# Own probability buffers for six attention units, a later first weight join, a slot table in two parts, and narrow slots scaled by VectorE

## The chip, the cores and the metric

The kernel runs on one core of a Trainium2 chip. The metric is the device time of one execution in microseconds (us). The engines are named as the profile names them: PE is TensorE's matrix multiply and PEld its weight load, DVE is VectorE, ACT ScalarE, POOL GpSimd, SP SyncE, which here only issues transfers. An engine carries out its instructions in the order in which they stand in its program; between engines only semaphores hold them.

## The reference

Three stages follow one another, on 2304 tokens of 512 values, in float32.

```python
scores = 0.125 * (q @ k.T)             # 4 batches x 8 heads, 576 x 576, head size 64
mask   = local (32 back) for heads 0-3, every 32nd position for heads 4-7
attn   = softmax(where(mask, scores, -1e9)) / (sum + 1e-9);  x = attn @ v
xn     = x / sqrt(mean(x*x) + 1e-6) * rms_g
x      = (silu(xn @ w_gate) * (xn @ w_val)) @ w_out           # 512 -> 1536 -> 512
logits = x @ w_gate2 + modality_bias[modality_id]             # 8 experts
e, p   = argmax(logits), softmax(logits)[argmax]
out    = p * (relu(x @ w1[e]) @ w2[e])                        # 512 -> 1024 -> 512
```

## The kernel before, in words

**Attention** is cut into 48 units (a batch, two heads, a group of blocks). `attention(u)` has four steps: `scores()` (matmuls L195 into a PSUM bank; DVE adds the mask and writes the probability buffer `pr`, L206; DVE takes the maxima, L214; ACT takes the exponent in place, L217), `norm()` (DVE: sum L237, reciprocal L240, product L241), `transpose()` (PE L247, into PSUM, and a copy) and `output()` (PE L258). `pr` comes from a pool of three buffers: the unit three further on can write its own only when PE has transposed this one. GpSimd writes a small constant into the last column of each `pr` (L184).

The first twelve units run ahead of all else (the loop over `aux`). In this prologue the weights of the first feed-forward are loaded and converted as well. 36 weights of 512 KB come packed by the ACT queue (`load_w`, L446) and are taken apart in three steps: `conv_a` (GpSimd takes the middle bits, L452), `conv_b` (DVE joins them in place, L456; the "join") and `conv_c` (ACT rounds the high part, L463, DVE subtracts to get the low part, L464). Weight 3f is the gate of hidden block f, 3f+1 the value, 3f+2 the output. `convert()` takes the next of these steps from a list; in the prologue it starts after step P1 of `aux`.

**First feed-forward.** Tokens go in nine chunks of 256. After a normalisation (`rms`: L367 to L403; y, xh, xl at L413 to L417), `gate_val` does 24 matmuls for each hidden block (L511 to L513), `gelu_post` is ACT and DVE (L519 to L525), `ff_out` six matmuls (L536 to L538), two blocks behind. Chunk 1 starts two blocks behind chunk 0 and takes the same weights. The scheduler of the framework sets the order of each engine's rows by priorities; the rest of the attention is strewn between.

**Router and sorted experts.** For the last chunk and all that follows, `tc.manual_schedule()` keeps the order as written. `route_s` ranks the tokens (its last matmul is L631), `route_g` builds `ab` on DVE (L662, L665), and `route_i` is four matmuls on `ab` (L677) and an addition (L681) that give the sorted token numbers. `tables()` (DVE) works out from the counts which expert and which rows each of the slots t = 1 to 15 has: the rows in `s_l` (L971 to L984), the expert numbers in `ei` (`tables2()`, L990 to L1006). `gather(t)` turns `s_l` into row numbers (DVE L1034 to L1043) and fetches the tokens (GpSimd L1046); `experts(t)` reads `ei`. The work of a slot is `mm1` (L1098 to L1100, a relu at L1109 and L1115 behind it) and `mm2` (L1128 to L1138); `split` parts the loaded weights (ACT h L1062, DVE l L1063). `finish(t)` scales the result by the router's probability and writes it out. Slots 1, 7, 8 and 9 are narrow (192 rows instead of 256); in their second block ACT copies half of the PSUM tile, DVE adds the other half (L1154) and ACT scales (L1155). The last slot (`half_pair`, L1190) has its own relu `rl` (L1204) on ACT, which PE waits for at L1210.

Of the kernel before, what the change touches and what calls it, by code (L numbers as in the profile page):

```python
# [52 lines left out]
def moe_kernel(  # L53
# [117 lines left out]
    def attention(u, banks):  # L171
# [7 lines left out]
        def scores():  # L179
            t = qkv_t.pop((u, 0))  # L180

            pr = pp.tile([128, 4, LK + 1], F32, tag="pr", name="pr", bufs=3)
            if u < 12:
                G.memset(pr[:, :n, nk:nk + 1], 1e-9)  # L184
            mx = sm.tile([128, 4], F32, tag="mx", name="mx")
            sd = sm.tile([128, 4], F32, tag="sd", name="sd")
            sps = banks("s")
            if 0 < u < 12:
                fill(sps[:, 384:], 10)
            sps = sps[:, :4 * LK].rearrange("p (t k) -> p t k", k=LK)  # L190
# [12 lines left out]
            first = 1 if local and g == 0 else 0  # L203
            for i0, i1, mask in ((0, first, m_loc0), (first, n, m_loc if local else m_str)):
                if i1 > i0:
                    V.scalar_tensor_tensor(  # L206
                        out=pr[:, i0:i1, :nk],
                        in0=sps[:, i0:i1, :nk],
                        scalar=-0.125,
                        in1=mask[:, :nk].unsqueeze(1).to_broadcast([128, i1 - i0, nk]),  # L210
                        op0=ALU.mult,
                        op1=ALU.add,
                    )
            V.tensor_reduce(out=mx[:, :n], in_=pr[:, :n, :nk], op=ALU.min, axis=AX.X)  # L214
            for i in range(n):
                pv = pr[:, i, :nk]
                act = A.activation(  # L217
                    out=pv,
                    in_=pv,
                    func=AF.Exp,  # L220
                    bias=mx[:, i:i + 1],
                    scale=-1.0,
                    accum_out=None if u < 12 else sd[:, i:i + 1],
                )
                if not flow_on:
                    mark[0] = act
# [240 lines left out]
    mark = [None]  # L467
    flow_on = []

    def next_load():  # L470

        if n_wl[0] < NP and mark[0] is not None:
            with tc.issue_after(mark[0].ins):
                load_w(n_wl[0])
            n_wl[0] += 1

    conv = [lambda: conv_a(0), lambda: conv_b(0)]
    for n in range(1, NP):
        conv += [lambda n=n: (conv_a(n), conv_c(n - 1)), lambda n=n: conv_b(n)]
    conv += [lambda: conv_c(NP - 1)]  # L480
# [398 lines left out]
    def first_tables():  # L879
# [30 lines left out]
    def tables():  # L910
        tl, ti, r, h, nx = (lt[n] for n in ("tl", "ti", "r", "h", "nx"))
        wd, excl, incl, u = (lt[n] for n in ("wd", "excl", "incl", "u"))
        w0, w1, s_l, ex, place = (lt[n] for n in ("w0", "w1", "s_l", "ex", "place"))
        hi = lt["m"][:, 2:3]
        iota1 = iota[:, 1:E + 1]
        wide = [128, NL, 2, E]
        t_b = place.unsqueeze(2).unsqueeze(3).to_broadcast(wide)

        def before(a):
            V.tensor_tensor(out=ex, in0=lt["lt"], in1=a.unsqueeze(1).to_broadcast([128, E, E]), op=ALU.mult)  # L920
# [47 lines left out]
        yield  # L968
        V.tensor_tensor(out=u, in0=lt["base"], in1=excl, op=ALU.subtract)
        yield  # L970
        V.tensor_tensor(out=w0, in0=excl.unsqueeze(1).to_broadcast(wide), in1=t_b, op=ALU.is_le)  # L971
        yield
        V.tensor_tensor(out=w1, in0=incl.unsqueeze(1).to_broadcast(wide), in1=t_b, op=ALU.is_gt)
        yield
        V.tensor_tensor(out=w0, in0=w0, in1=w1, op=ALU.mult)
        yield

        V.scalar_tensor_tensor(
            out=w1, in0=u.unsqueeze(1).to_broadcast(wide), scalar=-float(BIG), in1=w0, op0=ALU.add, op1=ALU.mult
        )  # L980
# [6 lines left out]
    def tables2():  # L987
        w0, w1, et, ei, m = (lt[n] for n in ("w0", "w1", "et", "ei", "m"))
        wide = [128, NL, 2, E]
        V.tensor_tensor(  # L990
            out=w1, in0=w0, in1=lt["e_l"].unsqueeze(1).unsqueeze(2).to_broadcast(wide), op=ALU.mult
        )
        yield
        V.tensor_reduce(out=et[:, 1:], in_=w1.rearrange("p t a e -> p t (a e)"), op=ALU.add, axis=AX.X)
        yield
        V.tensor_scalar(out=et[:, 1:], in0=et[:, 1:], scalar1=m[:, 1:2], scalar2=None, op0=ALU.add)
        yield
        V.tensor_copy(et[:, 0:1], m[:, 1:2])
        yield
        V.tensor_copy(ei[:, 0], et[:, 1:])  # L1000
        yield
        V.tensor_tensor(out=ei[:, 1], in0=et[:, 1:], in1=et[:, :NL], op=ALU.not_equal)
        yield
# [139 lines left out]
    def finish(t, blocks=(0, 1), halves=False):  # L1143
        go = lt[f"go{t % 2}"]
        for m in blocks:
# [5 lines left out]
            elif m and t in NARROW:  # L1151
                A.copy(y[:HALF], p[HALF:])
                y, p, rs = y[:HALF], p[:HALF], slice(0, HALF)
                V.tensor_tensor(out=y, in0=p, in1=y, op=ALU.add)  # L1154
                A.activation(out=y, in_=y, func=AF.Copy, scale=go[rs, m:m + 1])  # L1155
            elif m:
                A.activation(out=y, in_=p, func=AF.Copy, scale=go[:, m:m + 1])
            else:
                V.tensor_scalar(out=y, in0=p, scalar1=go[:, m:m + 1], scalar2=None, op0=ALU.mult)
# [133 lines left out]
    with tc.manual_schedule():  # L1293
# [11 lines left out]
            next(ranks)  # L1305
        weave(ranks, route_g(j), tables())
        mm1(0, 2, (1,))
        mm1(0, 3, relu=False)
        mm2(0, 0, (0,))
        route_i(j)  # L1310
        mm2(0, 0, (1,))
        gather(1)
        weave(tables2())
        relu_split(0, 3)
        ef = experts(1)
        for i in range(3):
# [125 lines left out]
```

## Time and profile before

| | us |
|---|---|
| median of 3 runs | 844.97 (843.8 to 845.02) |
| the profiled execution | 843.3 |
| its span, first to last instruction | 841.0 |
| PE busy | 819.3 (97%) |
| DVE busy | 520.1 (62%) |
| ACT busy | 382.3 (45%) |
| POOL busy | 88.7 (11%) |

2.3 us of the profiled execution lie outside its span. The mean granted TensorE clock is 0.988 of full speed. A busy PE is not PE at its peak, so a saving is looked for where PE stands still or runs at a lower clock: some 22 us in all.

### The profile page before, as it was taken

Reading aid. Unit: us, or ns where it says so; the run is one execution under the profiler, and the core shown is the slowest. Engines: PE = TensorE matmul, PEld = TensorE weight load, DVE = VectorE, ACT = ScalarE, POOL = GpSimd, SP = SyncE. Lnnn points to the kernel's source line nnn. Section 1 sums busy time; section 2 is a strip of 40 time slices with the busy share of each in tenths; the row PEclk is TensorE's granted clock in tenths of the full one; section 3 lists DMA queues with packets and bytes.
Section 4 is the critical chain, followed back from the end, with each engine's and each line's share of the span. In section 5 each row is a group of like instructions: output and inputs, shape, how many; then the busy total and the mean of one; then the engine's idle time right before and its main releaser. Section 6 shows DMA issues by size and latency. Waiting matters only on the chain. (4 is left out here: it accounts for less than half of the span.)

```text
span 841.0 us, 17627 instructions
## 1 busy us (share of the span) xinstructions
PE 819.3 (97%) x6746; PEld 740.9 (88%) x6746; DVE 520.1 (62%) x1433; ACT 382.3 (45%) x943; POOL 88.7 (11%) x103
## 2 busy tenths in 40 slices
PE   8799999999999999999999999999999999999995
PEld 7589989999988998899989999999989999999994
DVE  5989984544564554663554524538688666667762
ACT  5765564343553354542242322325365455545552
POOL 2424410000000000000000000001023111221201
PEclk9789999999999999999999999999999999999999
DMA  9969201011211111200000000006059667777773
GB/s 271 348 219 350 79 18 49 14 34 38 77 52 35 39 41 44 76 23 16 10 11 26 1 1 27 1 27 225 27 188 353 222 224 225 219 220 237 224 226 97
DMA packets 35587, 96.98 MB, mean 115 GB/s; under 512 B 4787, under 2 KB 12323, under 8 KB 35497
## 3 DMA queue, kind: packets, MB, share of 16 engines
q1 hardware_dynamic: 26520, 67.08, 25.2%
q10 hardware_dynamic: 5616, 19.07, 6.1%
q0 software_dynamic: 3360, 9.64, 3.5%
q8 instruction: 55, 0.90, 0.4%
q14 instruction: 36, 0.29, 0.1%
HBM read 91.04 MB, written 9.71 MB: 120 GB/s over the span
## 5 line engine op out<-in xcount | busy, mean ns | idle before, releaser
L511 PE MATMUL gv<-xh,wf 128*128 128x256 f32 x864 | 246.7, 287 | 0.9 <-DVE t L521 0.8
L512 PE MATMUL gv<-xl,wf 128*128 128x256 f32 x864 | 245.4, 284 | 0.3
L513 PE MATMUL gv<-xh,wf 128*128 128x256 f32 x864 | 244.9, 284 | 0.0
L511 PEld LDWEIGHTS gv<-xh,wf 128*128 128x128 f32 x864 | 163.3, 190 | 7.4 <-DVE t L521 1.6
L512 PEld LDWEIGHTS gv<-xl,wf 128*128 128x128 f32 x864 | 163.4, 189 | 5.0 <-DVE xl L417 0.9
L513 PEld LDWEIGHTS gv<-xh,wf 128*128 128x128 f32 x864 | 163.8, 190 | 0.5 <-issue 0.2
L1063 DVE TENSOR_TENSOR l<-stg,h 128x1024 fp32r<-128x1024 f32 x88 | 107.1, 1223 | 33.1 <-ACT h L1062 33.1
L1062 ACT CAST h<-stg 128x1024 fp32r<-128x1024 f32 x88 | 91.5, 1047 | 33.6 <-PE o L1130 13.3
L520 DVE SCALAR_TENSOR_TENSOR t<-t,gv 128x256 f32<-128x256 f32 x108 | 45.0, 417 | 86.0 <-ACT t L519 85.2
L519 ACT ACTIVATE t<-gv 128x256 f32<-128x256 f32 x108 | 41.1, 381 | 122.9 <-PE gv L513 109.2
L524 ACT CAST hh<-t 128x256 fp32r<-128x256 f32 x108 | 43.8, 405 | 77.4 <-DVE t L521 34.1
L536 PE MATMUL o<-wf,hh 128*128 128x512 f32 x192 | 77.0, 401 | 0.0
L537 PE MATMUL o<-wf,hh 128*128 128x512 f32 x192 | 76.2, 397 | 0.0
L538 PE MATMUL o<-wf,hl 128*128 128x512 f32 x192 | 74.9, 397 | 0.0
L525 DVE TENSOR_TENSOR hl<-t,hh 128x256 fp32r<-128x256 f32 x108 | 46.5, 430 | 34.4 <-ACT hh L524 33.3
L217 ACT ACTIVATE pr<-pr,mx 128x54 f32<-128x54 f32 (+1 forms) x160 | 52.4, 346 | 18.7 <-DVE mx L214 14.5
L1046 POOL DMA_INDIRECT xg<-rows_d,gi x22 | 24.2, 1100 | 299.0 <-DMA stg<-in 141.0
L1128 PE MATMUL o<-h,hT 128*128 128x512 f32 x128 | 51.9, 406 | 0.0
L1130 PE MATMUL o<-h,hT 128*128 128x512 f32 x128 | 50.1, 392 | 0.0
L1129 PE MATMUL o<-l,hT 128*128 128x512 f32 x128 | 49.8, 389 | 0.0
L521 DVE TENSOR_TENSOR t<-t,gv 128x256 f32<-128x256 f32 x108 | 44.9, 416 | 1.7
L1099 PE MATMUL s<-xl,h 128*128 128x256 f32 (+1 forms) x160 | 44.6, 279 | 0.3 <-DVE xl L1082 0.3
(267 smaller groups left out, 1560.6 us busy)
## 6 DMA issues: line engine op xcount, KB each, us to landing
stg<-in SPq DMA_DIRECT2D x96, 512.0 KB
raw<-in ACTq DMA_DIRECT2D x36, 511.8 KB
rows_d<-x SPq DMA_DIRECT2D x18, 256.5 KB
qk<-in SPq DMA_DIRECT2D x14, 221.0 KB
qk<-in SPq DMA_DIRECT2D x8, 272.0 KB
qk<-in SPq DMA_DIRECT2D x8, 208.0 KB
v<-in SPq DMA_DIRECT2D x14, 108.0 KB
qk<-in SPq DMA_DIRECT2D x7, 167.0 KB
```

The lines of the kernel that those rows point to most:

```text
L217: act = A.activation(out=pv, in_=pv, func=AF.Exp, bias=mx[:, i:i + 1], scale=-1.0, accum_out=None if u < 12 else sd[:, i:i + 1],)
L511: T.matmul(dst, wh[:, ks], xh[k], start=(k == order[0]), stop=False)
L512: T.matmul(dst, wh[:, ks], xl[k], start=False, stop=False)
L513: T.matmul(dst, wl[:, ks], xh[k], start=False, stop=(k == order[3]))
L536: T.matmul(o, h[:, ms], wh, start=(f == 0), stop=False)
L537: T.matmul(o, h[:, ms], wl, start=False, stop=False)
L538: T.matmul(o, l[:, ms], wh, start=False, stop=(f == NF - 1))
L1062: A.copy(h, lt["stg", i])
L1063: V.tensor_tensor(out=l, in0=lt["stg", i], in1=h.bitcast(F32), op=ALU.subtract)
L1128: T.matmul(ys[t][m], hh, w[0][:, c], start=(q == 0 and c == 0), stop=False)
L1129: T.matmul(ys[t][m], hh, w[1][:, c], start=False, stop=False)
L1130: T.matmul(ys[t][m], hl, w[0][:, c], start=False, stop=(q == 3 and c == 1))
```

## The change

- Units 0 to 5 get probability buffers of their own: slices of two tiles that later hold the weights 31 and 32 (`pr_early`). Unit 6 is the first to use the pool.
- `conv_b(0)` may be issued only behind the maxima of unit 6 (`first_join`), and `convert()` starts after step 15 of `aux` instead of 10.
- The slot table is built in two parts. `find(0, 2)` and `whose(0, 2)` stand where the whole table stood and do slots 1 and 2; `find(2, 15)`, `whose(2, 15)` and `count()` stand behind `split(7)`, ahead of `gather(3)`.
- In the written order `route_i` comes behind the first half of `mm1(0, 3)` instead of behind all of it and half of `mm2(0, 0)`, and `gather(1)` ahead of `mm2(0, 0)`.
- In `finish` of a narrow slot the first block goes from DVE to ACT, and the scaling of the second block from ACT to DVE.

```diff
-            pr = pp.tile([128, 4, LK + 1], F32, tag="pr", name="pr", bufs=3)
+            if u < 6:
+
+                if u % 3 == 0:
+                    pr_early[0] = wts.tile([128, 3, 4, SQ + 1], F32, tag=f"w{NP - 4 - u // 3}", name="pr_early")
+                pr = pr_early[0][:, u % 3]
+            else:
+                pr = pp.tile([128, 4, LK + 1], F32, tag="pr", name="pr", bufs=3)
...
+            masked[u] = V.tensor_reduce(out=mx[:, :n], in_=pr[:, :n, :nk], op=ALU.min, axis=AX.X)
...
+    def first_join():
+
+        with tc.issue_after(masked[6].ins):
+            conv_b(0)
...
-    conv = [lambda: conv_a(0), lambda: conv_b(0)]
+    conv = [lambda: conv_a(0), first_join]
...
-    P0, P1, P2, P3 = 3, 10, 1, 1
+    P0, P1, P2, P3 = 3, 15, 1, 1
...
+        yield from find(0, SOON)
+
+    def find(t0, t1):
...
+        V.tensor_tensor(out=w0, in0=excl, in1=t_b, op=ALU.is_le)
+        yield
+        V.tensor_tensor(out=w1, in0=incl, in1=t_b, op=ALU.is_gt)
+        yield
         V.tensor_tensor(out=w0, in0=w0, in1=w1, op=ALU.mult)
         yield
+        V.scalar_tensor_tensor(out=w1, in0=u, scalar=-float(BIG), in1=w0, op0=ALU.add, op1=ALU.mult)
+        yield
+        V.tensor_reduce(out=s_l, in_=w1.rearrange("p t a e -> p t (a e)"), op=ALU.add, axis=AX.X)
+        yield
+        V.scalar_tensor_tensor(out=s_l, in0=place, scalar=float(BIG), in1=s_l, op0=ALU.add, op1=ALU.add)
+        yield
...
                 V.tensor_tensor(out=y, in0=p, in1=y, op=ALU.add)
-                A.activation(out=y, in_=y, func=AF.Copy, scale=go[rs, m:m + 1])
-            elif m:
+                V.tensor_scalar(out=y, in0=y, scalar1=go[rs, m:m + 1], scalar2=None, op0=ALU.mult)
+            elif m or t in NARROW:
                 A.activation(out=y, in_=p, func=AF.Copy, scale=go[:, m:m + 1])
...
-        mm1(0, 3, relu=False)
-        mm2(0, 0, (0,))
+        mm1(0, 3, (0,))
         route_i(j)
-        mm2(0, 0, (1,))
+        mm1(0, 3, (1,), relu=False)
         gather(1)
-        weave(tables2())
+        mm2(0, 0)
+        weave(whose(0, SOON))
...
         split(7)
+        weave(find(SOON, NL))
+        weave(whose(SOON, NL), count())
         ef = experts(2)
```

`whose(t0, t1)` is `tables2()` on the columns t0 to t1, and `count()` its last two operations; one copy of `tables2()` moves to the tables that are set up beforehand.

The order of VectorE's rows in the prologue, before: the first join (`raw<-raw,top`) stands ahead of the scores of unit 5 (`pr<-s_386`), and the second behind all of unit 5.

```order
L237 TENSOR_REDUCE sd<-pr 128x4
L456 SCALAR_TENSOR_TENSOR raw<-raw,top 128x512
L206 SCALAR_TENSOR_TENSOR pr<-s_386,cs 128x3x54
...
L464 TENSOR_TENSOR wf<-raw,wf 128x512
L206 SCALAR_TENSOR_TENSOR pr<-s_441,cs 128x96
L206 SCALAR_TENSOR_TENSOR pr<-s_441,cs 128x3x96
L237 TENSOR_REDUCE sd<-pr 128x3
L214 TENSOR_REDUCE mx<-pr 128x4
L240 RECIPROCAL sd<-sd 128x3
L241 TENSOR_TENSOR pr<-pr,sd 128x3x54
L456 SCALAR_TENSOR_TENSOR raw<-raw,top 128x512
```

The same place of the changed kernel, whose lines are 9 further on (L465 is the join, L473 the subtraction of `conv_c`):

```order
L246 TENSOR_REDUCE sd<-pr_early 128x3
L215 SCALAR_TENSOR_TENSOR pr<-s_426,cs 128x96
L215 SCALAR_TENSOR_TENSOR pr<-s_426,cs 128x3x96
L249 RECIPROCAL sd<-sd 128x3
L223 TENSOR_REDUCE mx<-pr 128x4
L465 SCALAR_TENSOR_TENSOR raw<-raw,top 128x512
L250 TENSOR_TENSOR pr_early<-pr_early,sd 128x3x54
L465 SCALAR_TENSOR_TENSOR raw<-raw,top 128x512
...
L473 TENSOR_TENSOR wf<-raw,wf 128x512
```

The first join now stands behind the scores and maxima of units 5 and 6, and the second join only one row behind the first. Up to the start of the first feed-forward (the first `y<-x` row) before has eight joins and seven subtractions on VectorE, the changed kernel five and five.

Further on, VectorE's rows between the second gelu (`t<-t,gv`) of chunk 0 and the normalisation of chunk 1 (`y<-x`), before and then changed. In the first, the subtraction is that of weight 7; in the second, the joins are those of weights 5 and 6, and the subtraction that of weight 5.

```order
L464 TENSOR_TENSOR wf<-raw,wf 128x512
L456 SCALAR_TENSOR_TENSOR raw<-raw,top 128x512 x2
L520 SCALAR_TENSOR_TENSOR t<-t,gv 128x256
L464 TENSOR_TENSOR wf<-raw,wf 128x512
L521 TENSOR_TENSOR t<-t,gv 128x256
L413 SCALAR_TENSOR_TENSOR y<-x_752,g_sb,r 128x192
```

```order
L534 SCALAR_TENSOR_TENSOR t<-t,gv 128x256
L404 SCALAR_TENSOR_TENSOR nr<-nt,nr 128x2
L465 SCALAR_TENSOR_TENSOR raw<-raw,top 128x512 x2
L535 TENSOR_TENSOR t<-t,gv 128x256
L422 SCALAR_TENSOR_TENSOR y<-x_733,g_sb,r 128x192
...
L422 SCALAR_TENSOR_TENSOR y<-xs,g_sb,r 128x256 x2
L473 TENSOR_TENSOR wf<-raw,wf 128x512
L539 TENSOR_TENSOR hl<-t,hh 128x256
L465 SCALAR_TENSOR_TENSOR raw<-raw,top 128x512
```

Three joins and two subtractions thus stand behind the start of the feed-forward, and the output and gate weights 5, 6 and 7 are whole only behind chunk 1's `y`.

The third place is VectorE behind `split(7)` (the five `l<-stg,h`), in the changed kernel; before, the `pick` of `gather(3)` followed at once.

```order
L1088 TENSOR_TENSOR l<-stg,h 128x1024 x5
L992 TENSOR_TENSOR w_7508<-excl,place 128x208
L994 TENSOR_TENSOR w_7509<-incl,place 128x208
...
L1009 TENSOR_TENSOR w_7509<-w_7508,e_l 128x208
...
L1023 TENSOR_TENSOR ei<-et 128x13
L1059 SCALAR_TENSOR_TENSOR pick_7486<-iota,s_l,ids 128x144
...
L1184 TENSOR_SCALAR y_8275<-o_8097,go_7479 128x512
L1140 SCALAR_TENSOR_TENSOR hT<-s_8303,hT 128x2x64
```

Thirteen rows have come in ahead of the `pick`, of the scaling of slot 0's first block (`y`) and of the first relu row of slot 1 (`hT`).

## Rows read from the trace of the kernel before

**Rows 1.** The page: busy time of the engines, and granted TensorE clock by slices.

```profile
PE 819.3 (97%) x6746; PEld 740.9 (88%) x6746; DVE 520.1 (62%) x1433; ACT 382.3 (45%) x943; POOL 88.7 (11%) x103
...
PEclk9789999999999999999999999999999999999999
```

**Rows 2.** Windows: stretch: us, busy PE, PEld, DVE, ACT, POOL, clock, DMA share, GB/s.

```profile
25.00:30.00 5.00, 3.05 (x50) 2.46 (x50) 5.00 (x11) 3.64 (x11) 3.03 (x4) 1.00 1.04 397
30.00:35.00 5.00, 3.17 (x35) 2.10 (x37) 5.00 (x12) 3.86 (x11) 3.20 (x5) 0.67 1.01 390
...
40.00:45.00 5.00, 4.54 (x49) 3.25 (x49) 3.52 (x13) 3.09 (x10) 0.00 (x0) 0.50 0.21 57
45.00:50.00 5.00, 5.00 (x37) 4.61 (x37) 2.99 (x8) 2.61 (x14) 0.00 (x0) 0.62 0.21 60
```

**Rows 3.** Timeline of DVE and POOL, 16 to 21 us: start, duration, row, [idle before].

```profile
16.47 0.69 DVE L456 SCALAR_TENSOR_TENSOR raw<-raw,top 128x512 int32<-128x512 int32 x1 [1.71 <-POOL pr L184]
...
20.71 0.68 DVE L456 SCALAR_TENSOR_TENSOR raw<-raw,top 128x512 int32<-128x512 int32 x1
...
19.90 0.76 POOL L452 CAST top<-raw 128x512 f16<-128x512 bf16 x1 [3.42 <-DMA raw<-in]
```

**Rows 4.** Timeline of the ACT queue: the second load of a packed weight.

```profile
12.43 0.33 ACTq L446 DMA_DIRECT2D raw<-in  x1
```

**Rows 5.** Timeline of DVE and PE: start of the first feed-forward.

```profile
42.42 0.88 DVE L413 SCALAR_TENSOR_TENSOR y<-x,g_sb,r 128x256 f32<-128x256 f32 x2 [1.19 <-ACT r L403]
...
44.80 0.79 PE L511 MATMUL gv<-xh,wf 128*128 128x256 f32 x2
```

**Rows 6.** Timeline of DVE and PE, 64 to 67 us: weight 10 whole; gate of block 3.

```profile
64.53 0.68 DVE L464 TENSOR_TENSOR wf<-raw,wf 128x512 fp32r<-128x512 f32 x1
...
66.92 0.38 PE L511 MATMUL gv<-xh,wf 128*128 128x256 f32 x1
```

**Rows 7.** Timeline of PE and DVE around `route_i`, 605 to 609 us.

```profile
605.67 0.28 PE L1098 MATMUL gv<-xh,h 128*128 128x256 f32 x1
...
608.48 0.42 PE L677 MATMUL mx<-ab 128*128 128x144 bf16 x4
...
606.93 0.28 DVE L665 TENSOR_SCALAR ab<-iota,sc 128x144 bf16<-128x144 f32 x1
```

**Rows 8.** Timeline of DVE and PE, 608 to 632 us: the slot table, and slot 1.

```profile
608.29 0.40 DVE L971 TENSOR_TENSOR w<-excl,place 128x240 f32<-128x240 f32 x1
...
610.37 0.17 DVE L984 SCALAR_TENSOR_TENSOR s_l<-place,s_l 128x15 f32<-128x15 f32 x1
...
612.41 0.40 DVE L990 TENSOR_TENSOR w<-w,e_l 128x240 f32<-128x240 f32 x1
...
613.96 0.15 DVE L1006 TENSOR_SCALAR more<-cf 128x1 int32<-128x1 f32 x1
...
617.71 0.55 PE L1077 MATMUL pt<-cs,xg 128*128 128x128 f32 x3 [0.47 <-DMA xg<-rows_d,gi]
...
620.46 0.35 PE L1099 MATMUL s<-xl,h 128*128 128x192 f32 x1 [0.30 <-DVE xl L1082]
...
628.57 0.74 DVE L1159 TENSOR_SCALAR y<-o,go 128x512 f32<-128x512 f32 x1
...
631.15 0.42 PE L1128 MATMUL o<-h,hT 128*128 128x512 f32 x1
```

**Rows 9.** Timeline of ACT and PE, 820 to 825 us: the last narrow slot, then `half_pair`.

```profile
820.44 0.58 ACT L1152 COPY y<-o 64x512 f32<-64x512 f32 x1
822.97 0.72 ACT L1155 ACTIVATE y<-y,go 64x512 f32<-64x512 f32 x1 [1.94 <-DVE y L1154]
823.71 0.66 ACT L1204 ACTIVATE rl<-s 128x256 f32<-128x256 f32 x2
...
822.12 0.28 PE L1202 MATMUL s<-l,xh 128*128 128x256 f32 x1
824.15 0.44 PE L1210 MATMUL pt<-cs,rl 128*128 128x128 f32 x2 [1.75 <-ACT rl L1204]
```

More of the change, by code (lines that the diff above doesn't have):

```diff
@@ L45 @@
 HALF = 64
+SOON = 2
 L_COLS = [2 * LQ * n + WIN for n in L_TILES]
@@ L118, in moe_kernel @@
     v_pair = [None]
+    pr_early = [None]
+    masked = {}
     n_out = [0]
@@ L213, in scores @@
                     )
-            V.tensor_reduce(out=mx[:, :n], in_=pr[:, :n, :nk], op=ALU.min, axis=AX.X)
+            masked[u] = V.tensor_reduce(out=mx[:, :n], in_=pr[:, :n, :nk], op=ALU.min, axis=AX.X)
             for i in range(n):
@@ L904, in first_tables @@
         V.tensor_scalar(out=lt["e_l"], in0=iota8, scalar1=mf, scalar2=None, op0=ALU.subtract)
+        V.tensor_copy(lt["et"][:, 0:1], mf)
         for slots, at_ in ((WIDE[1:], 0), (NARROW, 16), ((BASE - 1,), 32), (range(BASE, NP2), len(WIDE) - 1)):
@@ L912, in tables @@
         wd, excl, incl, u = (lt[n] for n in ("wd", "excl", "incl", "u"))
-        w0, w1, s_l, ex, place = (lt[n] for n in ("w0", "w1", "s_l", "ex", "place"))
+        ex = lt["ex"]
         hi = lt["m"][:, 2:3]
         iota1 = iota[:, 1:E + 1]
-        wide = [128, NL, 2, E]
-        t_b = place.unsqueeze(2).unsqueeze(3).to_broadcast(wide)
         def before(a):
@@ L970, in tables @@
         yield
-        V.tensor_tensor(out=w0, in0=excl.unsqueeze(1).to_broadcast(wide), in1=t_b, op=ALU.is_le)
+        yield from find(0, SOON)
+    def find(t0, t1):
+        n = t1 - t0
+        excl, incl, u = (lt[i].unsqueeze(1).to_broadcast([128, n, 2, E]) for i in ("excl", "incl", "u"))
+        w0, w1, s_l, place = (lt[i][:, t0:t1] for i in ("w0", "w1", "s_l", "place"))
+        t_b = place.unsqueeze(2).unsqueeze(3).to_broadcast([128, n, 2, E])
+        V.tensor_tensor(out=w0, in0=excl, in1=t_b, op=ALU.is_le)
         yield
-        V.tensor_tensor(out=w1, in0=incl.unsqueeze(1).to_broadcast(wide), in1=t_b, op=ALU.is_gt)
+        V.tensor_tensor(out=w1, in0=incl, in1=t_b, op=ALU.is_gt)
         yield
@@ L976, in tables @@
         yield
-        V.scalar_tensor_tensor(
-            out=w1, in0=u.unsqueeze(1).to_broadcast(wide), scalar=-float(BIG), in1=w0, op0=ALU.add, op1=ALU.mult
-        )
+        V.scalar_tensor_tensor(out=w1, in0=u, scalar=-float(BIG), in1=w0, op0=ALU.add, op1=ALU.mult)
         yield
@@ L985, in tables, with whose, count @@
         yield
-    def tables2():
-        w0, w1, et, ei, m = (lt[n] for n in ("w0", "w1", "et", "ei", "m"))
-        wide = [128, NL, 2, E]
+    def whose(t0, t1):
+        n, m = t1 - t0, lt["m"]
+        w0, w1, et, ei = lt["w0"][:, t0:t1], lt["w1"][:, t0:t1], lt["et"], lt["ei"]
         V.tensor_tensor(
-            out=w1, in0=w0, in1=lt["e_l"].unsqueeze(1).unsqueeze(2).to_broadcast(wide), op=ALU.mult
+            out=w1, in0=w0, in1=lt["e_l"].unsqueeze(1).unsqueeze(2).to_broadcast([128, n, 2, E]), op=ALU.mult
         )
         yield
-        V.tensor_reduce(out=et[:, 1:], in_=w1.rearrange("p t a e -> p t (a e)"), op=ALU.add, axis=AX.X)
+        V.tensor_reduce(
+            out=et[:, t0 + 1:t1 + 1], in_=w1.rearrange("p t a e -> p t (a e)"), op=ALU.add, axis=AX.X
+        )
         yield
-        V.tensor_scalar(out=et[:, 1:], in0=et[:, 1:], scalar1=m[:, 1:2], scalar2=None, op0=ALU.add)
+        V.tensor_scalar(
+            out=et[:, t0 + 1:t1 + 1], in0=et[:, t0 + 1:t1 + 1], scalar1=m[:, 1:2], scalar2=None, op0=ALU.add
+        )
         yield
-        V.tensor_copy(et[:, 0:1], m[:, 1:2])
+        V.tensor_copy(ei[:, 0, t0:t1], et[:, t0 + 1:t1 + 1])
         yield
-        V.tensor_copy(ei[:, 0], et[:, 1:])
+        V.tensor_tensor(
+            out=ei[:, 1, t0:t1], in0=et[:, t0 + 1:t1 + 1], in1=et[:, t0:t1], op=ALU.not_equal
+        )
         yield
-        V.tensor_tensor(out=ei[:, 1], in0=et[:, 1:], in1=et[:, :NL], op=ALU.not_equal)
-        yield
+    def count():
         V.tensor_reduce(out=lt["cf"], in_=lt["wd"][:, 0], op=ALU.add, axis=AX.X)
```

## The prediction

> **What bounds the kernel now.** I read the page first: PE is busy 819.3 of 841.0 us [rows 1], so no edit can win more than some 22 us unless it takes PE's work away, and this one takes none. The line of the granted clock shows where PE is slow besides: two slices near the start and nowhere else. The windows say what happens there [rows 2]: from 25 to 35 us VectorE is busy without a gap while PE works 3.05 and 3.17 of 5 us; then the clock falls, from 1.00 to 0.67 and 0.50, and in 40 to 50 us it is still 0.50 and 0.62 although PE is full again. So the prologue is VectorE's, and the start of the first feed-forward pays for it twice. From 45 us on PE is the bound, and a saving of another engine counts only at the few rows where PE waits. The lists of rows show three that this change touches: the waits around slot 1's transposes [rows 8], the spare time before slot 1's `mm2` [rows 8], and 1.75 us at the end, where PE waits for the relu of the last slot [rows 9].
>
> **Prologue (own buffers, later join).** Before, VectorE stands still for 1.71 us in front of the first join, with unit 5 queued behind it [rows 3]. The row names GpSimd's constant, which had to wait for a free `pr`. In the changed order units 5 and 6 fill that gap, so I let the first join stay at about 16.5. But the second join now stands one row behind it, at about 17.4, and it needs GpSimd's cast of raw(1). That cast ran at 19.90 and ended at 20.66, and what ended its wait was the load [rows 3]. The load was issued at 12.43, behind unit 3's exponents [rows 4]; with unit 3 no longer waiting I put the issue 1.2 us earlier. How much of this reaches the landing no row shows: all of it gives 19.4 for the join, none of it 20.7, and if the cast had besides been late behind other POOL work, 18.2. I take 19.0, nearest to the full shift. So a new wait of 1.6 us (0.8 to 3.3) takes the place of the old 1.71. At the end of the second join VectorE is ahead by 20.71 - 19.0 less 0.6 for the first subtraction, not yet done: 1.1 us (-0.6 to 1.9).
>
> The Trainium skill (DMA: Bandwidth & Descriptors, Issuing engines are not separate DMA queues) says that transfers issued by different engines run on the same 16 DMA engines and interleave. The trace agrees in that the DMA share is 1.01 to 1.04 here [rows 2]. By that rule an earlier issue adds no bandwidth, and the landing would stay; the sum would then go by the 20.7 above.
>
> Three joins and two subtractions move behind the start of the feed-forward. At 0.64 us from row to row that is 3.2 us, so the first dense matmul, at 44.80 [rows 5], should come at about 44.8 - 3.2 - 1.1 = 40.5. This is not the gain, because the moved work is late next. The changed order has PE use the output weight 5 and the gate weights 6 and 7 behind both first gelus, and VectorE joins them only there. Further on the chase goes on: ahead of weight 10's subtraction stand 17 rows that stood behind it before (half a unit of attention, one join, one gelu row and five router constants). By their spacings these are 4.4 us. Against it stand the 1.1 us and what is filled of VectorE's pauses at 40 to 50 us (10 less 3.52 and 2.99 is 3.5 us [rows 2]; the 1.19 us for `r` [rows 5] stays, and of the rest I count 1.0 as filled, since VectorE soon waits for PE's gate sums again). Weight 10 was whole at 64.53 + 0.68 = 65.2 [rows 6]; it will be at 65.2 + 4.4 - 1.1 - 1.0 = 67.5. PE needs its low part at the fifteenth matmul of block 3's gate, 66.92 + 14 x 0.12 = 68.6 before [rows 6]. So PE can be 1.1 us ahead there and no more, whatever happened at 40 us: **-1.1 us**. With the bounds of the join the same sum gives -1.9 to +0.6. If nothing gates, the whole 4.3 us could stay.
>
> **Slot table and `route_i`.** PE now meets `route_i` 24 matmuls behind the ranks, at 605.67; the last `ab` is whole at 606.93 + 0.28 = 607.21 [rows 7]. PE waits 1.5 us where it waited for nothing (L677 at 608.48 came late enough). In return `gather(1)` is about 2 us earlier, which takes away the 0.47 us for the gathered tokens, and the transposes come in time to take away the 0.30 us for `xl` [rows 8]; with the break in pipelining I count 1.0. Net +0.5.
>
> The later table costs thirteen VectorE rows of 208 instead of 240 columns. The same rows before took from 608.29 to 610.46 and from 612.41 to 614.03, less 0.12 for the copy that moved [rows 8]: 3.7 us, and scaled by the columns of the wide ones 3.4 (2.8 if no row waits for the one ahead). They stand ahead of slot 0's scaling `y`, which was done at 628.57 + 0.74 = 629.31, and of slot 1's relu. PE's `mm2` needs `y`'s bank at 631.15 [rows 8]: 1.84 us to spare. VectorE comes there about 0.45 us earlier, since the transposes no longer hold `xl`. So `mm2` starts 3.4 - 0.45 - 1.84 = 1.1 us later than before; the +0.5 of `route_i` lies inside this wait. **+1.1 us** (0.3, if VectorE gains 1.2 us ahead of it, to 1.9). Slot 3's expert number is ready before its weight buffers are free, so no load waits. The shorter first table saves nothing by itself: VectorE waits for loads after it anyway.
>
> **Narrow slots.** Before the last slot ACT copies (820.44), waits 1.94 us for VectorE's sum, scales (822.97 + 0.72) and only then does `rl`; PE is through at 822.12 + 0.12 and waits until 824.15 [rows 9]. After, ACT scales block 0 (about 0.66, as its 0.72 row with the same columns), copies (0.58) and goes on to `rl` at about 821.7, ready at 822.1. PE's wait nearly goes: 824.15 - 822.3 = **-1.8 us** (-1.2, if ACT starts late behind its cast, to -1.9). VectorE takes one scaling off and one on. Slots 7 and 8 gain nothing, as PE has other matmuls there.
>
> **Sum:** -1.1 + 1.1 - 1.8 = -1.8 us on the profiled 843.3, so 841.5. That run is 1.7 us below the median of the three; on the median's scale I predict 843.2.
>
> **Rivals.**
> 1. *The clock falls once in the new gaps.* PE will wait for weights 5, 6 and 7 between about 50 and 60 us and then be about as busy as at 25 to 35 us, where the clock fell [rows 2]; against it, attention's matmuls stand in the same stretch. After 44.80 [rows 5] a full PE still ran at half speed until about 48.8 (that gives the mean of 0.62 in 45 to 50 us [rows 2]), which is 2 us lost. PE would reach block 3's gate 2 us later, some of which the wait for weight 10 hides: +0.5 instead of -1.1, in all 844.8. The Trainium skill (TensorE: Matmul & The Clock Gate, HAM oscillation) tells that bursts with waits between them bring the slower clock back each time; by it this rival would be the rule, and the time 844.8 or more.
> 2. *Slower: the clock stays at 1.2 GHz until weight 10 is there.* It decides if PE never gets a full run between 50 and 68 us. Then a second restoration of 2 us comes behind the wait for weight 10 and nothing hides it: +2.5 + 1.1 - 1.8 = +1.8, 846.8. For it: at 45 us PE was full and still at 0.50. Against: 24 gate matmuls of chunk 1 need no new weight.
> 3. *The change doesn't do what it says: raw(1) lands no earlier.* The old wait is merely replaced, the join is at 20.7: +0.6 + 1.1 - 1.8, 844.9. For it the full DMA share [rows 2].
> 4. *Nothing gates.* If VectorE's order leaves weight 10 in time, the 4.3 us at the start stay: -4.3 + 1.1 - 1.8 = -5.0, 840.0.
> 5. *The later table is hidden*, because VectorE gets to it 1.2 us sooner: -1.1 + 0.3 - 1.8 = -2.6, 842.4.
>
> **How the numbers follow.** A measurement of this kernel tells about 0.2%, 1.7 us, from no change. Chances: my sum 0.42 (it lies at the border: 0.24 faster, 0.18 same), rival 1 0.13 (same), rival 2 0.13 (slower), rival 3 0.10 (0.08 same, 0.02 slower), rival 4 0.12 (faster), rival 5 0.10 (faster). Faster 0.46, same 0.39, slower 0.15. The range leaves out about half of rival 4 and half of rival 2: 840.4 to 846.6; my sum by itself has 842.0 to 844.8.
>
> **What would show it.** Right: no wait of VectorE for GpSimd's constant at the first join, but one for raw at the second; the first dense matmul at 39 to 42 us; PE waiting between 50 and 60 us for rows of `conv_c`; PE waiting 1.3 to 1.7 us at L691 and about 0.6 us ahead of slot 1's `mm2`; L1235 directly behind the last L1227. Wrong: a first dense matmul no earlier than 44 us, a clock below 1.00 after 50 us, weight 10 no later than 66 us, or no wait ahead of slot 1's `mm2`.

## The result, and the profile after

The changed kernel takes 851.86 us (median of 4 runs, 850.53 to 853.54) against 844.38 us before it (4 runs on the same chip, 843.04 to 845.02): ratio 1.0084 [1.0061, 1.0107]. It is slower by about 7.5 us, where 1.8 us less were forecast, and it lies outside the range. The profiled execution took 853.54 us with a span of 851.3.

The page, as in [rows 1]: the slices of the clock show three slow ones in a row near the start, not two.

```profile
PE 824.7 (97%) x6746; PEld 746.6 (88%) x6746; DVE 521.5 (61%) x1444; ACT 380.5 (45%) x943; POOL 87.7 (10%) x103
...
PEclk9777999999999999999999999999999999999999
```

Three rows place the loss. The last matmul of the rank sums before `route_i` (L631) starts at 602.71 before and 613.81 after: 11.1 us are lost by then, and all of them before 85 us: at 82 us PE is 12.3 us late, and 1.2 of these come back on the way. From L631 to the first matmul of slot 1's `mm2` the later table costs 1.18 us more, and at the end 1.9 us come back.

The windows of the changed kernel (columns as in [rows 2]) show where in the prologue:

```profile
20.00:25.00 5.00, 3.26 (x66) 2.57 (x62) 4.57 (x11) 4.22 (x12) 2.33 (x3) 0.99 1.03 313
25.00:30.00 5.00, 3.59 (x30) 3.08 (x32) 3.26 (x8) 2.06 (x6) 0.90 (x3) 0.50 0.90 296
30.00:35.00 5.00, 3.92 (x51) 2.88 (x47) 3.43 (x10) 3.36 (x11) 1.96 (x4) 0.82 0.84 266
35.00:40.00 5.00, 3.47 (x49) 2.84 (x50) 4.34 (x16) 3.52 (x11) 0.00 (x0) 0.86 0.96 354
...
45.00:50.00 5.00, 4.64 (x43) 4.14 (x42) 3.86 (x11) 4.32 (x18) 0.00 (x0) 0.50 0.43 117
50.00:55.00 5.00, 5.00 (x36) 5.00 (x35) 2.79 (x14) 1.97 (x10) 0.00 (x0) 0.78 0.18 43
...
70.00:75.00 5.00, 0.70 (x6) 0.33 (x4) 5.00 (x14) 3.09 (x11) 2.33 (x3) 0.77 0.68 242
75.00:80.00 5.00, 5.00 (x42) 4.67 (x43) 5.00 (x9) 2.57 (x6) 1.66 (x2) 0.50 1.03 406
80.00:85.00 5.00, 5.00 (x28) 4.64 (x27) 4.93 (x11) 3.00 (x12) 2.24 (x3) 0.70 0.48 131
```

Two things are to be seen. VectorE, which before had no gap from 20 to 35 us [rows 2], now pauses, 4.40 us between 20 and 40 us. And from 70 to 75 us PE does almost nothing while VectorE is full.

A sum that I use below: PE's busy time times the granted clock, summed over the ten windows from 40 to 90 us, is the work done, in us at full clock. It is 45.0 before and 32.9 after. The difference, 12.1, is the delay that PE carries out of this stretch: the third output product starts at 69.84 before (L536) and at 82.16 after (L550), 12.3 later. By parts, 2.7 of the 12.1 fall in 40 to 55 us, 1.0 in 55 to 70, 4.5 in 70 to 75, and 4.0 in 75 to 85, where PE is full at a lower clock.

The joins, against [rows 3, 4] (timeline of VectorE, GpSimd and the ACT queue):

```profile
16.64 0.68 DVE L465 SCALAR_TENSOR_TENSOR raw<-raw,top 128x512 int32<-128x512 int32 x1
20.23 0.69 DVE L465 SCALAR_TENSOR_TENSOR raw<-raw,top 128x512 int32<-128x512 int32 x1 [2.67 <-POOL top L461]
...
19.43 0.77 POOL L461 CAST top<-raw 128x512 f16<-128x512 bf16 x1 [2.94 <-DMA raw<-in]
...
11.51 0.33 ACTq L455 DMA_DIRECT2D raw<-in  x1
```

The old wait of 1.71 us is gone and one of 2.67 us stands at the second join. The load of raw(1) was issued 0.92 us earlier and its cast began 0.47 us earlier. The start of the first feed-forward, against [rows 5] (timeline of VectorE and PE):

```profile
26.41 0.91 PE L204 MATMUL s<-qk 64*64 64x96 f32 x8 [3.11 <-DMA qk<-in]
...
43.46 0.88 DVE L422 SCALAR_TENSOR_TENSOR y<-x,g_sb,r 128x256 f32<-128x256 f32 x2 [1.18 <-ACT r L412]
...
46.24 0.80 PE L525 MATMUL gv<-xh,wf 128*128 128x256 f32 x2 [0.36 <-ACT xh L425]
```

It comes 1.4 us later than before, not 4.3 earlier. Then PE's waits from 40 to 90 us, the largest of them (engine, tile and line, what was waited for: us in total, times, longest). Before, the two largest of this stretch were 0.4 and 0.2.

```profile
PE gv L525 <- DVE t L535: 2.5, 1, 2.5
PE mx L256 <- DVE sd L249: 1.8, 1, 1.8
PE gv L410 <- DVE nr L404: 1.5, 1, 1.5
```

And what stands around the largest, on VectorE, ACT and PE (timelines; before this gate began at 66.92 [rows 6]):

```profile
67.34 0.68 DVE L473 TENSOR_TENSOR wf<-raw,wf 128x512 fp32r<-128x512 f32 x1
...
71.80 1.10 DVE L473 TENSOR_TENSOR wf<-raw,wf 128x512 fp32r<-128x512 f32 x1
72.83 0.41 DVE L534 SCALAR_TENSOR_TENSOR t<-t,gv 128x256 f32<-128x256 f32 x1
...
73.45 0.68 DVE L465 SCALAR_TENSOR_TENSOR raw<-raw,top 128x512 int32<-128x512 int32 x1
74.06 0.41 DVE L534 SCALAR_TENSOR_TENSOR t<-t,gv 128x256 f32<-128x256 f32 x1
74.39 0.41 DVE L535 TENSOR_TENSOR t<-t,gv 128x256 f32<-128x256 f32 x1
74.72 0.73 DVE L473 TENSOR_TENSOR wf<-raw,wf 128x512 fp32r<-128x512 f32 x1
...
70.83 0.37 ACT L533 ACTIVATE t<-gv 128x256 f32<-128x256 f32 x1
...
71.94 0.49 PE L256 MATMUL mx<-cs,pr 128*54 128x128 f32 x3 [1.78 <-DVE sd L249]
74.94 0.55 PE L525 MATMUL gv<-xh,wf 128*128 128x256 f32 x1 [2.52 <-DVE t L535]
...
80.03 0.41 PE L527 MATMUL gv<-xh,wf 128*128 128x256 f32 x1
```

Before, weight 7 and the end of block 2's gelu (timeline of VectorE):

```profile
54.35 0.68 DVE L464 TENSOR_TENSOR wf<-raw,wf 128x512 fp32r<-128x512 f32 x1
...
64.20 0.41 DVE L521 TENSOR_TENSOR t<-t,gv 128x256 f32<-128x256 f32 x1
```

The gate of block 3 writes a `gv` bank, of which there are two, and the gelu of block 2 frees it. That gelu now stands on VectorE between the conversions of weights 9 and 10 (L473 at 71.80 and 74.72). Weight 10 is whole at 75.45, and PE comes to its low part, with the fifteenth matmul from 74.94 on, only at 80.03: it waits for the gelu, not for this weight. The gelu is late from further back. Block 2 needs weight 7, which was whole at 55.03 and is now whole at 68.02 (L473 at 67.34). Block 2's sums end at about 70.2 (58.4 before), ACT starts its part of the gelu at 70.83, and VectorE's product ends at 74.80 (64.61 before).

Around `route_i` and slot 1, against [rows 7, 8] (timelines of PE and VectorE): two short waits at L691 instead of one long one, no wait left for the gathered tokens or for `xl`, and 0.88 us ahead of `mm2`.

```profile
617.16 0.55 PE L691 MATMUL mx<-ab 128*128 128x144 bf16 x2 [0.22 <-DVE ab L679]
618.10 0.50 PE L691 MATMUL mx<-ab 128*128 128x144 bf16 x2 [0.39 <-DVE ab L679]
643.43 0.47 PE L1153 MATMUL o<-h,hT 128*128 128x512 f32 x1 [0.88 <-DVE y L1184]
...
642.54 0.75 DVE L1184 TENSOR_SCALAR y<-o,go 128x512 f32<-128x512 f32 x1
```

The end, against [rows 9] (timelines of ACT and PE): ACT goes from its copy straight to `rl`, and PE's 1.75 us are gone.

```profile
832.63 0.69 ACT L1182 ACTIVATE y<-o,go 128x512 f32<-128x512 f32 x1
833.34 0.58 ACT L1177 COPY y<-o 64x512 f32<-64x512 f32 x1
833.95 0.38 ACT L1229 ACTIVATE rl<-s 128x256 f32<-128x256 f32 x1
...
834.47 0.28 PE L1227 MATMUL s<-l,xh 128*128 128x256 f32 x1
834.59 0.38 PE L1235 MATMUL pt<-cs,rl 128*128 128x128 f32 x2
```

### The profile page after: what moved, and what is told of

Read it like the earlier page. It is cut to its first block, busy times and chain, and to the rows that moved or that the text cites. A ratio compares the mean times of both kernels' runs of the same rounds, so it can differ in the third digit from the quotient of the medians.

```text
span 851.3 us, 17630 instructions
## 1 busy us (share of the span) xinstructions
PE 824.7 (97%) x6746; PEld 746.6 (88%) x6746; DVE 521.5 (61%) x1444; ACT 380.5 (45%) x943; POOL 87.7 (10%) x103
## 4 chain that ended last, share of the span: by engine, by line
PE 80%; issue 6%; DVE 5%; DMA 5%; ACT 1%; POOL 1%; SPq 1%; ACTq 0%; POOLq 0%; DVEq 0%
PE gv L525 11%; PE gv L526 11%; PE gv L527 11%; PE o L551 5%; PE o L550 5%; PE o L552 5%; PE o L1153 3%; PE o L1155 3%; PE o L1154 3%; PE mx L267 2%; PE s L1123 2%; PE s L1124 2%; PE s L1125 2%; PE s L204 2%; PE gv L1123 2%
## 5 line engine op out<-in xcount | busy, mean ns | idle before, releaser
L538 ACT CAST hh<-t 128x256 fp32r<-128x256 f32 x108 | 43.8, 405 | 75.3 <-DVE t L535 33.4
L550 PE MATMUL o<-wf,hh 128*128 128x512 f32 x192 | 77.1, 402 | 0.3 <-ACT hh L538 0.3
L226 ACT ACTIVATE pr<-pr,mx 128x96 f32<-128x96 f32 (+1 forms) x138 | 46.8, 349 | 13.3 <-DVE mx L223 12.6
L1123 PE MATMUL s<-xh,h 128*128 128x256 f32 (+1 forms) x160 | 44.6, 279 | 0.0
```

Of the source, the lines that this page charges most:

```text
L550: T.matmul(o, h[:, ms], wh, start=(f == 0), stop=False)
L1123: T.matmul(dst, w[0][:, k, cs_], xh, start=(k == 0), stop=False)
```

## The experiments

**The change taken apart.** Theory: the prologue part alone loses the time, and the other two parts do what the sum said. Rival: the table or `route_i` does it. First the prologue part alone (own buffers, first join behind unit 6's maxima, 15 for 10), then the table and the narrow slots alone.

```diff
+            if u < 6:
...
+                if u % 3 == 0:
+                    pr_early[0] = wts.tile([128, 3, 4, SQ + 1], F32, tag=f"w{NP - 4 - u // 3}", name="pr_early")
+                pr = pr_early[0][:, u % 3]
...
-    conv = [lambda: conv_a(0), lambda: conv_b(0)]
+    conv = [lambda: conv_a(0), first_join]
...
-    P0, P1, P2, P3 = 3, 10, 1, 1
+    P0, P1, P2, P3 = 3, 15, 1, 1
```

> Only the edits of the prologue (own buffers, first join behind unit 6's maxima, conversions from step 15); table, route_i and narrow slots as before. If the loss is the prologue's and passes through PE's dense part undiminished, 8 to 10 us slower than before. Rival, that the later parts cost some of it (a table that is late on VectorE, a changed order around route_i): clearly less, 4 to 6 us slower.

Measured: 850.83 against 844.78 us, 1.0074 [1.0049, 1.0099]: +6.05 us. The first dense matmul comes at 43.44, even 1.4 us before that of the kernel before, and yet the third output product starts 9.7 us late (79.58): this loss arises behind the start. Its windows (columns as in [rows 2]):

```profile
65.00:70.00 5.00, 2.98 (x25) 2.53 (x23) 5.00 (x15) 3.46 (x14) 1.96 (x2) 1.00 0.24 47
70.00:75.00 5.00, 2.65 (x28) 2.46 (x29) 5.00 (x11) 2.89 (x8) 1.64 (x2) 0.54 1.02 415
75.00:80.00 5.00, 5.00 (x31) 4.81 (x28) 5.00 (x10) 3.48 (x13) 1.53 (x2) 0.50 0.71 251
```

VectorE is full in all three. Work by the sum above: 34.9, that is 10.1 less than before.

```diff
+        yield from find(0, SOON)
...
-        weave(tables2())
+        weave(whose(0, SOON))
...
+        weave(find(SOON, NL))
+        weave(whose(SOON, NL), count())
...
-                A.activation(out=y, in_=y, func=AF.Copy, scale=go[rs, m:m + 1])
+                V.tensor_scalar(out=y, in0=y, scalar1=go[rs, m:m + 1], scalar2=None, op0=ALU.mult)
```

> Only the other edits (slot table in two parts, route_i earlier, narrow slots); prologue as before. By the sum of the prediction +1.1 - 1.8 = -0.7 us (-1.6 to +0.4). Rival, that they hold part of the loss: slower by 2 us or more.

Measured: 845.0 us, 1.0003 [0.9986, 1.0019], no difference that the timing shows. The traces agree to 602.71 us (L631), so from there on they can be laid side by side: slot 1's `mm2` waits 0.88 us for `y`; PE's last L1202 ahead of L1210 starts 1.27 us later than before (823.39 against 822.12), and PE's last matmul starts 0.71 earlier (832.52 against 833.23). The forecast's two terms gave +1.1 - 1.8 = -0.7.

**The prologue part taken apart.** Theory: the five conversion steps that moved behind the dense start (15 for 10) make the loss. Rivals: the buffers, whose space is that of later weights; or the join's new place.

```diff
...
+                pr = pr_early[0][:, u % 3]
...
```

> Only the own probability buffers; conversions from step 10 and the first join free, as before. If the buffers do what they are for and the late join is what costs, faster by 1 to 4 us, with the first dense matmul before 44 us and no wait of VectorE in front of the first join for GpSimd's constant. Rival, that the buffers bring the loss (units 3 to 5 run ahead, and the queues of loads get into another order): 5 us slower or more.

Measured: 846.28 us, 1.0016 [0.9998, 1.0035]. The buffers alone bring nothing and cost 0 to 3 us.

```diff
...
-    conv = [lambda: conv_a(0), lambda: conv_b(0)]
+    conv = [lambda: conv_a(0), first_join]
...
-    P0, P1, P2, P3 = 3, 10, 1, 1
+    P0, P1, P2, P3 = 3, 15, 1, 1
```

> Only the later join and the conversions from step 15; probability buffers from the pool, as before. If the late join costs, 5 to 12 us slower, with conversions behind the start of the feed-forward and PE waiting between 55 and 80 us. Rival, that it is the buffers: within 2 us of before.

Measured: 852.73 us, 1.0104 [1.0067, 1.0142]: the loss stands without the buffers.

```diff
-    P0, P1, P2, P3 = 3, 10, 1, 1
+    P0, P1, P2, P3 = 3, 15, 1, 1
```

> Only one number: conversions from step 15 instead of 10; pool buffers and a free first join as before. Theory: the loss comes from five conversion steps that move behind the start of the feed-forward, where VectorE has no room for them; then 5 to 9 us slower, with PE waiting behind block 2's and block 3's gates. Rival: the loss needs the wait behind unit 6's maxima (raw(1) late with units queued behind it); then within 2 us of before.

Measured: 851.62 against 843.94 us, 1.0090 [1.0073, 1.0107]: this one number alone loses 7.7 us. Its first dense matmul is at 47.28, later than before: fewer conversions ahead of it did not bring it forward. `convert()` issues loads too, so this number moves some of them as well. But in the changed kernel GpSimd's casts wait from 45 to 85 us for VectorE's joins (15.2 us in eleven waits) and for no load.

On top of the prologue part, the next one takes two conversions at a step for steps 18 to 22, so that as many joins (8) and subtractions (7) stand ahead of the dense start as before the change.

```diff
-            convert()
+            convert(2 if 18 <= n_p < 23 else 1)
```

> The prologue's edits as in e1, but at five places two conversion steps are taken instead of one, so that eight joins and seven subtractions stand ahead of the feed-forward again. Theory of the moved steps: PE's gap behind the third gate goes and the time is within 3 us of before. Rival, that the late first join costs by itself: still 5 us or more slower, the first dense matmul later than 47 us.

Measured: 846.53 us, 1.0037 [1.0023, 1.0052]: 3.5 of the 6.05 us come back, and 2.6 stay. What stays arises ahead of the gap: the first dense matmul is 1.7 us late (46.53), the third output product 1.6 (71.45) and the last L631 1.8 (604.49). VectorE's order is that of before again too, by the subtractions ahead of each of the first eight gelus: twelve ahead of the fourth, for one, where the prologue part alone has ten. So this run gives back the count and the order together. Its window 70 to 75 us, where the prologue part alone had PE at 2.65 and a clock of 0.54:

```profile
70.00:75.00 5.00, 4.80 (x35) 4.19 (x34) 5.00 (x16) 2.88 (x10) 1.16 (x2) 1.00 1.01 391
```

**What is late there: VectorE's work, its order, or the clock.** Three theories: VectorE has too much to do up to about 80 us; it does the right amount in the wrong order (gelu behind conversions); or the gap is short and the lower clock after it is the loss. Each is changed by itself on top of the prologue part. The first has VectorE subtract 64 of 512 columns for weights 5 to 12.

```diff
-        V.tensor_tensor(out=w[:, 1], in0=wk, in1=w[:, 0].bitcast(F32), op=ALU.subtract)
+        if 5 <= n <= 12:
+            G.memset(w[:, 1, 64:].bitcast(F32), 0.0)
+            V.tensor_tensor(out=w[:, 1, :64], in0=wk[:, :64], in1=w[:, 0, :64].bitcast(F32), op=ALU.subtract)
```

> The prologue's edits as in e1, but the subtraction for the low parts of weights 5 to 12 does 64 of 512 columns (GpSimd writes zeros into the rest, so these low parts are left out of the result). That takes some 0.5 us each from VectorE. If PE's gap is VectorE's backlog of conversions, 4 us or more of e1's 6 us come back. Rival, that loads of weights or the clock at the start hold PE: less than 1.5 us comes back.

Measured: 844.54 us, 0.9999 [0.9986, 1.0011]: the whole loss is gone. The same edit on the kernel before was not run, but it had little to win there: PE is busy for all but 0.34 us from 50 to 90 us, at a clock of 1.00. In its window 70 to 75 us VectorE has room and PE keeps its clock:

```profile
70.00:75.00 5.00, 4.26 (x34) 3.93 (x31) 4.23 (x11) 2.85 (x12) 2.96 (x5) 1.00 0.99 327
```

The second lets PE multiply constants ahead of block 3's gate, so that it is not idle in the gap.

```diff
+            if n == 4:
+                fill(bank("mx")[:, :128], 100)
```

> The prologue's edits as in e1, and 100 small matmuls on constants (some 0.055 us each) ahead of the fourth block's gate, most of which PE does while it would wait. If the clock that falls in the gap holds a good part of the loss, the granted clock stays 1.00 from 65 to 90 us and 2 to 4 us of e1's 6 us come back. Rival, that the wait alone is the loss: no change from e1, or up to 3 us slower by the added matmuls.

Measured: 849.07 us, 1.0065 [1.0041, 1.0090]. The clock stays at 1.00:

```profile
70.00:75.00 5.00, 5.00 (x53) 4.76 (x51) 4.96 (x10) 2.06 (x4) 2.29 (x4) 1.00 1.00 401
75.00:80.00 5.00, 5.00 (x65) 4.76 (x64) 4.97 (x9) 3.32 (x7) 3.24 (x3) 1.00 0.84 307
```

By the medians some 1 us of the 6 comes back (5.1 against 6.05 above the kernel before, each beside its own runs), by the last PE matmul of the two traces 2.9 (838.48 against 841.33). The two runs' intervals overlap, so the first figure is not clear of noise. By the last L631 of the traces the delay falls from 8.1 to 5.2 us (607.95 against 602.71 before). So the half clock is a part of the loss, some 1 to 3 us, and not all of it. From 64 to 95 us this trace has no wait of PE at all: where PE would wait for VectorE it does the added matmuls, which themselves bring the result no further.

The third holds the conversions back behind the gelus of (0, 2) and (1, 0).

```diff
-        V.tensor_tensor(out=t, in0=t, in1=v, op=ALU.mult)
+        done = V.tensor_tensor(out=t, in0=t, in1=v, op=ALU.mult)
+        if (j, f) in ((0, 2), (1, 0)):
+            hold[0] = done
```

> The prologue's edits as in e1, but the conversions behind block 2's gelu (chunk 0) may be issued only behind its products, so that this gelu no longer stands behind the steps of weights 8 to 10. If what holds PE is the gate's PSUM bank, which that gelu reads late, 2 to 5 us of e1's 6 us come back. Rival, that the missing weights hold PE anyway: less than 1 us comes back, and PE waits for the subtractions of weights 9 and 10.

Measured: 848.53 against 844.69 us, 1.0045 [1.0027, 1.0064]: 2.2 of the 6.05 us come back, by medians whose intervals overlap. The third output product is in time (68.93; here PE does it ahead of block 3's gate, before it came behind), but the fifth is 9.0 late (87.66 against 78.67). The gap moved on to the gate of block 4, and PE waits there for a gelu's product again. No weight is missing: the fourteen subtractions up to weight 13 are done at 80.38, ahead of that gelu. Its window 80 to 85 us and PE's row:

```profile
80.00:85.00 5.00, 2.88 (x13) 2.91 (x14) 5.00 (x11) 2.46 (x6) 1.66 (x2) 0.70 1.00 403
...
82.12 0.55 PE L525 MATMUL gv<-xh,wf 128*128 128x256 f32 x1 [2.40 <-DVE t L535]
```

**The other direction.** If fewer conversions ahead of the start cost time, do more gain it? Two rivals stood, one of a gain and one of a small loss.

```diff
-    P0, P1, P2, P3 = 3, 10, 1, 1
+    P0, P1, P2, P3 = 3, 6, 1, 1
```

> Only one number, the other way: conversions from step 6 instead of 10; all else as before. VectorE then has two conversion steps more ahead of the feed-forward, 1 to 3 us. If the balance between prologue and feed-forward is what decides, within 2 us of before or up to 2 us faster, with no PE wait behind the third gate. Rival, that each step ahead of the feed-forward delays its start one for one: 1.5 to 3 us slower.

Measured: 856.23 us, 1.0140 [1.0110, 1.0169]. Both were wrong by far. The edit moves four steps and not two: ten joins and nine subtractions stand ahead of the start. The first dense matmul is 8.0 us late (52.79), and the same wait stands at 82.69, again for gelu's product (timelines of VectorE and PE):

```profile
80.08 0.68 DVE L464 TENSOR_TENSOR wf<-raw,wf 128x512 fp32r<-128x512 f32 x1
...
80.97 0.41 DVE L520 SCALAR_TENSOR_TENSOR t<-t,gv 128x256 f32<-128x256 f32 x1
...
82.69 0.58 PE L511 MATMUL gv<-xh,wf 128*128 128x256 f32 x1 [3.02 <-DVE t L521]
```

Here VectorE is not behind with its weights. Sixteen subtractions, up to weight 15, stand ahead of that gelu, the fourth (80.97); before it is twelve, in the changed kernel ten. So the place of a gelu behind conversions can cost PE such a wait by itself.

Of 6, 10 and 15 the value before, 10, is the best, and the others lose 11.5 and 7.7 us.

**What of the change is worth keeping.** The narrow slots alone:

```diff
-                A.activation(out=y, in_=y, func=AF.Copy, scale=go[rs, m:m + 1])
-            elif m:
+                V.tensor_scalar(out=y, in0=y, scalar1=go[rs, m:m + 1], scalar2=None, op0=ALU.mult)
+            elif m or t in NARROW:
```

> Only the narrow slots' edit (first block scaled by ScalarE, second by VectorE); all else as before. By the prediction's term 1.8 us faster (1.2 to 1.9), all of it at the last slot's first transposes, which come directly behind the last matmul of its first part. Rival, that the rest of the end chain gives it back: no change.

Measured: 843.35 against 844.69 us, 0.9979 [0.9959, 0.9998]; L1210 follows the last L1202 without a wait. The same with the table in two parts, but three slots early and the rest behind slot 1's steps:

```diff
...
+SOON = 3
...
+            if t == 1:
+                weave(find(SOON, NL))
+                weave(whose(SOON, NL), count())
```

> The table, route_i and narrow slots as changed, prologue as before, but the first part of the table does slots 1 to 3 and the second part stands behind slot 1's steps instead of ahead of gather(3). If the 1.1 us of the later table come from its place ahead of slot 0's scaling, the wait ahead of slot 1's mm2 goes and the time is 1.3 to 2.0 us below before. Rival, that the second part holds up something wherever it stands: 0.7 us below before, as in e2's sum, or slower.

Measured: 843.03 us, 0.9984 [0.9970, 0.9999]. Slot 1's `mm2` starts with no wait:

```profile
634.14 0.42 PE L1147 MATMUL o<-h,hT 128*128 128x512 f32 x1
```

From the last L631 to that L1202 (L1221 in this kernel) it takes 219.60 us, against 219.41 before and 220.68 with the table where the change put it. With the narrow slots alone, whose rows up to there are those of before, it takes 220.09, so single traces differ by 0.7 us here; the wait of 0.88 us that is gone is the surer figure for the place of the later table. No gain is left of splitting it. Both versions beat the kernel before, by some 1.5 us with intervals that end just below 1, and the change by more; they cannot be told from each other.

## Why the prediction was wrong

**Where it was right.** The table: +1.18 us measured for +1.1, by the mechanism named, `y` behind the thirteen rows. The narrow slots: -1.9 for -1.8, `rl` straight behind ACT's copy. The wait at `route_i` was too large: 0.6 us in two pieces, since the first two `ab` let PE begin, instead of 1.5; as it lies inside the later wait it changed nothing. Of the prologue, the new wait at the second join came, at its later bound (2.67 us of 0.8 to 3.3).

**The step that failed** is the term of the prologue, -1.1: "So PE can be 1.1 us ahead there and no more." Measured alone it is +6.05. Two estimates in it were too good, the 1.1 was a small difference between them, and the weight that it followed was not what PE came to wait for.

*The start.* "The first dense matmul, at 44.80, should come at about 40.5." That took VectorE for the bound right up to the start, so that each row taken away would bring it forward. Measured: 43.44 with the prologue part alone and 46.24 in the whole change. One prologue does not always run alike: five traces with this one start at 43.44 to 46.24, four with that of before at 44.80 to 47.93. By the means the start is 1.5 us earlier, not 4.3. What is missing can be counted in the two traces. The second join came at 19.76 and 20.23, not at 19.0, which is 0.8 and 1.2 us. And VectorE now idles from 20 to 40 us: 2.5 us and 4.4 us by the windows, where before it idled 0.07. 40.5 + 0.8 + 2.5 = 43.8, and 40.5 + 1.2 + 4.4 = 46.1. The rows taken away turned into pauses, in which VectorE waits for PE and ACT, and PE for loads of the attention units (the 3.11 us at 26.41 above). That these units could go no faster than they did is what my sum left out; which of their waits comes first differs between the two traces and was not settled.

*The chase.* From the dense start to weight 10 whole I allowed 27.0 us (20.4 before, 4.4 and 3.2 more, 1.0 for filled pauses). Measured: 29.4 with the prologue part alone (43.44 to 72.86) and 29.2 in the whole change (46.24 to 75.45). No pause was filled: with the prologue part alone VectorE was busy 10.2 of the 15 us from 40 to 55 us, less than the 10.9 before. The moved conversions stand in program order behind the first gelus, so they could not use the time in which VectorE stood still ahead of them.

Together these make weight 10 late by 2.9 + 2.4 = 5.3 us against 67.5 in the one case and by 5.7 + 2.2 = 7.9 in the other. PE's slack was spent to 1.1 us by my own sum.

*The wait.* I looked only for weight 10, and late as it was, PE did not wait for it. PE stopped ahead of it, for the `gv` bank that the gelu of block 2 frees, and came to weight 10's low part 4.6 us after it was whole (80.03 against 75.45). I had named the weights 6 and 7 as late and not followed them: weight 7 came 13.0 us later than before, and with it block 2's sums (11.7 us), its gelu (10.2) and the gate of block 3 (8.0, 74.94 against 66.92). Behind the gap comes the lower clock, and the third output product is 12.3 us late.

**What is shown, and what is not.** Shown is that the moved conversion steps make the loss (15 for 10 alone loses 7.7 us; with the steps given back to the prologue the gap goes) and that PE waits for VectorE's rows (with less work on VectorE all of the loss goes, 0.9999). Not shown is whether VectorE's amount of work up to about 80 us is the cause or its order. Shorter subtractions also shorten what stands ahead of each gelu, and the steps given back bring the old order back too. Putting two gelus first gave 2.2 us, which is not clear of noise, and the next gap was again a gelu behind conversions. The start at 6 speaks against the amount alone: there the weights were early, and PE waited for a gelu all the same.

**The rivals.** Rival 2 had the sign, but not the mechanism. The clock did fall again, as rival 1 said, but at 70 to 80 us and not between 50 and 60: 0.77 and 0.50 in the changed kernel, 0.54 and 0.50 with the prologue part alone, behind a gap. The Trainium skill (TensorE: Matmul & The Clock Gate, HAM oscillation) tells of just that, and these windows agree. But with the clock held at 1.00 only about 1 to 3 us came back. Rival 3's premise held by half: of 0.92 us in the issue 0.47 reached the cast, at a DMA share of 1.02 to 1.04 from 10 to 25 us (the rows that I had gone by were of 25 to 35 us). The Trainium skill's rule (DMA: Bandwidth & Descriptors, Issuing engines are not separate DMA queues) agrees with this. By the join alone it would have cost 1.7 us against my sum; the rest of the loss had nothing to do with it. Rivals 4 and 5 did not come to pass.

**Open.** The prologue part alone costs 6.05 us in the medians and the table and the narrow slots about nothing, while the whole costs 7.5; the intervals cover the 1.4 between them, and whether the parts act on each other was not tried. Why the first dense matmul comes 8.0 us late with the start at 6, and whether the 2.6 us that stay with the count of before are more than the spread of such starts (below), was not settled. A run that changes only the order of gelus and conversions, for all blocks, would tell amount from order.

## What to carry to other kernels

Work that is moved off the engine that bounds one stage must be followed to where it lands: here it landed in a stage in which the same engine had no room, and its place in program order kept it from using the pauses on the way. A small gain that is left between two large terms is no forecast; check first whether the stage that is relieved really ends sooner, by listing the waits that take over when the busy engine gets shorter. And where an accumulator bank is freed by an engine that works in order, whatever is queued ahead of that freeing step belongs to the path.

## What the runs showed that I had not expected

The same prologue does not always run alike. The two kernels whose prologue is that of before, the narrow slots alone and the table behind slot 1, had their first dense matmul at 46.69 and 47.93 in their profiled runs, where the kernel before and the table and narrow slots alone had 44.80 and 44.97, and the clock of 25 to 30 us was 0.50 in the second of them, with PE busy for all 5.00 us, where it was 1.00 before. The third output product was up to 2.5 us later (72.31 against 69.84). So a difference of up to 3 us in the prologue of single profiles says nothing here; the losses of the change, of its prologue part and of the starts at 15 and 6 are larger, and every run of these kernels lies above every run of the kernel before beside it.

A full PE at half clock hides in the busy column: from 75 to 80 us it reads 5.00 of 5.00 in the changed kernel and is worth 2.5. Busy time times granted clock found the 12.1 us at once; busy time alone (49.2 us before and 42.0 after, from 40 to 90) shows 7.2 of them.
